# Layer 0 of a Strassen-tiled cross network: one fused VectorE instruction for the state, and product 3 cut into seven

## The chip, the cores and the metric

The kernel runs on one core of a Trainium2 chip. The metric is the device time of one execution, in microseconds, as the median of several runs. Before the change it is 2269.24 us (three runs, 2269.07 to 2269.5). The engines are called by their names in the profile: PE is TensorE's matmul, PEld its weight load, DVE is VectorE, ACT is ScalarE, POOL is GpSimd, SP is SyncE, which here issues all DMAs.

## The reference

The inputs are x0 (16384 x 1024), six weight matrices ws (1024 x 1024 each) and six bias rows bs, all bfloat16. What is computed is

```python
x = x0
for l in range(6):
    proj = x @ ws[l] + bs[l]
    x = x0 * proj + x
```

In layer 0, x is x0, so the new state is x0 * proj + x0.

## The kernel before

**Tiles.** 1024 rows of x make a pair: two column blocks of 512 rows each, held transposed, features on partitions. A pair's state is one "big" tile (128 x 2 x 8 x 512: which of the two blocks, which of eight groups of 128 features, which row of the block). Eight sweeps (the loop over s) each take two pairs, side A and side B, through the six layers, in the order A0, B0, A1, B1 and so on: 96 steps. There are six big tiles: x0 of A and of B, the states of A and of B, and two for the next sweep's x0. "home" says which is which; they change roles at each sweep.

**Products.** A step multiplies the pair by a layer's weights as one level of a Strassen-Winograd scheme: seven products of half matrices, numbered 1 to 7, instead of eight. Each half product is 16 matmuls with 512 columns (4 row tiles by 4 of the contraction), in `mm`. The combined weights (5, 6, 7, 3) are made once, in sweep 0, by `combo` on VectorE, and stored to a DRAM tile Lc; from sweep 1 on they are loaded into a ring of nine weight tiles "wp" by `prefetch_upto`, on SP's queue. The combined activations are T13 (T5 and T7 in one tile), T2 (for product 6) and T4 (for product 4); each is a VectorE difference, in tiles of one buffer each.

**Products within products.** Product 2 in nearly all steps (`in2`) and product 4 from sweep 1 on (`in4`) are again cut in the same way: seven 256x256 products of four 256-column matmuls each, in `inner`. They need the differences of the activations (four VectorE instructions of 512 elements, `inner_t`, tiles ti2 and ti4, one buffer each) and of the weights (combo 8 for product 2, combo 9 for product 4, each four VectorE instructions of 512 elements and a store to Lc). Their partial results leave PSUM through ScalarE casts (`evi`) into ea, eb (product 2) and e4, e5 (product 4), and VectorE adds them up: for product 4 `s4` (two of 512 elements) and one of 2048 that adds E4 to C2.

**PSUM and ScalarE.** There are two pools of four PSUM banks, "px"; their roles change each step. Bank after bank is evicted by ScalarE, in program order: a cast (`acopy`) or an activation with the bias (`abias`), into P1s, P5s, S53, U2s (one buffer each) and C2 ("cb", two buffers). A new use of a bank waits for the eviction of the old one. In products 2 and 4, and between P1, P6 and P7, matmuls go on adding to a bank that ScalarE has read in between.

**The state.** A quarter of a new state is product sum times x0, plus the old state. So a quarter costs VectorE a multiplication and an addition (`fin_of`, 2048 elements each); the last two quarters (C2) are done in one multiplication and one addition of 4096 elements. The first quarter is made at the end of its own step (m0, a0). The others are the trail: they are done on VectorE at the head of the next step, between that step's own T2, T4 and ti4 (`trail`; the names in the loop are m1, s11, a1, s4, e4, mC2, aC2). s11 adds P5s to a half of C2, which is the last read of P5s. Before the step ends VectorE also makes ti2 of the other side (j02, j1, j3).

**Order.** `pin` keeps VectorE's, ScalarE's and SP's instructions in the order in which the program makes them. The matmuls are not pinned; the scheduler may interleave those of neighbouring products. In sweep 0 the weights are combined between the other work: in step A0 `combo(0, 8)` and `combo(0, 9)`, in step B0 those of layer 1. A `combo` on "ti4" uses the same single buffer as the activations' ti4.

**SP's queue.** Loads of weights wait for a free slot of the ring. At the end of a sweep, `turn_pair` transposes a state by DMA into the pair's old x0 tile and `write_pair` stores it, two DMAs of 1 MB; these stand in `pending`, which is issued at the head of a step after the prefetches.

Of the kernel before, what the change touches and what calls it, by code (L numbers as in the profile page):

```python
# [8 lines left out]
ADD = mybir.AluOpType.add  # L9
# [8 lines left out]
def kernel(  # L18
# [26 lines left out]
    def vtt(out, in0, in1, op):  # L45
        return pin(nc.vector.tensor_tensor(out=out, in0=in0, in1=in1, op=op))  # L46

    def vcopy(out, in_):
        return pin(nc.vector.tensor_copy(out=out, in_=in_))

# [25 lines left out]
    def bank(p):  # L76
        return p.tile([P, NB], FP32, name="px")

    Lc = dram.tile([L, 6, P, KH * H], BF16, name="Lc")
    CIDX = {5: 0, 6: 1, 7: 2, 3: 3, 8: 4, 9: 5}  # L80
    lc = lambda l, pid: Lc[l, CIDX[pid]].rearrange("p (k e) -> p k e", k=KH)

    def raw_src(l, pid):
# [38 lines left out]
    def combo(l, pid):  # L122
        if pid <= 7:
            a, op, b = {5: (lambda: raw12[l], ADD, lambda: W[0, l, 4]), 6: (lambda: W[0, l, 5], SUB, lambda: W[0, l, 1]),
                        3: (lambda: W[0, l, 2], SUB, lambda: W[0, l, 6]), 7: (lambda: W[0, l, 1], SUB, lambda: raw12[l])}[pid]
            if pid == 5:
                W[0, l, 5] = ei_pool.tile([P, KH, H], BF16, name=("eb", "e4")[l % 2])
            t = W[0, l, pid]
            vtt(t[:], a()[:], b()[:], op)
        else:  # L130
            w = W[0, l, {8: 2, 9: 4}[pid]]
            t = W[0, l, 8] if pid == 8 else ti_pool.tile([P, KH, H], BF16, name="ti4")
            i11, i12, i21, i22 = w[:, 0:2, 0:HE], w[:, 0:2, HE:H], w[:, 2:4, 0:HE], w[:, 2:4, HE:H]
# [5 lines left out]
        pin(nc.sync.dma_start(lc(l, pid), t[:]))  # L139
# [4 lines left out]
    def inner_t(hold, src, name):  # L144

        def t02():
            ti = ti_pool.tile([P, 4, 2, NQ], BF16, name=name)
# [12 lines left out]

        return [t02, t1, t3]
# [39 lines left out]
    make_identity(nc, ident[:])  # L201
    b_rows = const.tile([LK, P], BF16, name="b_rows")
    b_all = const.tile([P, LK], FP32, name="b_all")
    ones = const.tile([P, P], BF16, name="ones")
    signs = const.tile([P, P], BF16, name="signs")
    nc.vector.memset(ones[:], 0.0)
    nc.vector.memset(ones[0:1, :], 1.0)
    nc.vector.memset(signs[:], 0.0)
    nc.vector.memset(signs[0:2, :], 1.0)
    nc.vector.memset(signs[0:1, :], -1.0)  # L210
# [50 lines left out]
    def trail(Y, store):  # L261

        if Y is None:
            return [None] * 7
        C2, E4, e5 = Y.C2, Y.E4, Y.e5
        eh1 = lambda t: t[:, :, KH:KD, :]
        m1, a1 = fin_of(Y, Y.C12, 0, 1)

        def s4():
            for i in range(2):  # L270
                vtt(E4[:, 2 * i:2 * i + 2, NQ:NB], E4[:, 2 * i:2 * i + 2, (1 - i) * NQ:(2 - i) * NQ], e5[:], ADD)

        def a1s():
            a1()
            if store:
                store_half(Y, 0)

        return [m1, lambda: vtt(C2[:, 1], C2[:, 1], Y.P5s[:], ADD), a1s,
                s4 if E4 is not None else None,
                (lambda: vtt(C2[:, 0], C2[:, 0], E4[:], ADD)) if E4 is not None else None,  # L280
                lambda: vtt(C2[:], C2[:], eh1(Y.x0T), MULT),
                lambda: vtt(eh1(Y.xst), C2[:], eh1(Y.src_in), ADD)]

    def fin_of(Y, C, eh, n):
        xs = half(eh)
        return [lambda: vtt(C, C, Y.x0T[:, n, xs, :], MULT),
                lambda: vtt(Y.xst[:, n, xs, :], C, Y.src_in[:, n, xs, :], ADD)]

# [39 lines left out]
    for s in range(NPAIR // 2):  # L328
        for l in range(L):
            for side in ("A", "B"):  # L330
                X, Y = cur[side], prev
                first, last = step == 0, (X.pr, l) == LAST
                in2, in4 = not first, s > 0 and not (s + 1 == NPAIR // 2 and l + 1 == L)
                psA, psX = ps[step % 2], ps[1 - step % 2]
                step += 1
                bias = lambda eh, m, l=l: b_all[:, l * KD + eh * KH + m: l * KD + eh * KH + m + 1]
                if l == 0:
                    if side == "A" and s > 0:
                        home = dict(xA=home["nA"], xB=home["nB"], sA=home["sA"], sB=home["sB"], nA=home["xA"], nB=home["xB"])
                    X.xst = bigt(home["s" + side])  # L340

                def bring(who, s=s, home=home):
                    pr = 2 * (s + 1) + (who == "B")
# [9 lines left out]
                if s + 1 == NPAIR // 2 and side == "A" and l == 2:  # L353
                    x0R = bigt(home["nA"])[:].rearrange("p n k b -> p (n k b)").rearrange("p (j d) -> p j d", d=D)
                    xsR = bigt(home["nB"])

                    def load_rows():
                        pin(nc.sync.dma_start(brow[:], bs[L - 1].rearrange("(h e) -> h e", h=2)))
                        pin(nc.sync.dma_start(x0R, x0[B - PR:B, :].rearrange("(j p) d -> p j d", p=P)))

                    brow = zero[0:2, :]
                    pending.append(load_rows)

                def end_of(Y, late):
                    if s + 1 == NPAIR // 2 and side == "A" and l == L - 1 and not late:
# [19 lines left out]
                def mm(pid, wt, pts, m, start):  # L385
                    rhs = X.rhs(pid)
                    if last:
                        pt = pts[m][:]
                        if pid == 1:
                            nc.tensor.matmul(pt, lhsT=ones[:], rhs=zero[:], start=True, stop=False)  # L390
                        elif pid == 7:
                            nc.tensor.matmul(pt, lhsT=signs[:], rhs=zero[:], start=False, stop=False, skip_group_check=True)
# [30 lines left out]
                m1, s11, a1, s4, e4, mC2, aC2 = trail(Y, ended and last)  # L423
                if not first:
                    X.T13()
                P1s = evt("P1s")
# [11 lines left out]
                for f in (m1, s11, a1, t2, s4, t4, e4, i02, mC2, i1, aC2, i3):  # L438
                    if f is not None:
                        f()  # L440
                if in2:
                    q2, q5, q1 = bank(psX), bank(psX), bank(psX)
                    w2i = weights(8)
# [44 lines left out]
                    ev(P5s, pX, 3)  # L488
                    ev(S53, pX, 0, 0)
                    ev(P1s, pA, 3, 0)  # L490
                    for m in range(1, KH):
                        mm(3, w3, pX, m, False)
                        ev(S53, pX, m, 0)
# [57 lines left out]
                if s == 0:  # L551
                    if side == "A":
# [20 lines left out]
                X.C2, X.P5s, X.l = C2, P5s, l  # L573
                if in4:
                    w4, w4i, w7 = weights(4), weights(9), weights(7)
                    wj, wr4 = w4i[:].rearrange("p k (j e) -> p k j e", e=HE), sub_w(w4, HE)
# [15 lines left out]
                    inner(cols(z1), wj[:, 1], t4[:, 1], False)  # L592
                    evi(e4[0, 1], z1)
                    mm(6, w6, pA, 3, False)
                    ev(U2s, pA, 3)
                    mm(7, w7, pA, 0, False)
                    ev(C2[:, 1], pA, 0, 1)
                    inner(cols(z1), wj[:, 3], t4[:, 2], False)
                    evi(e4[1, 0], z1)
                    for m in range(1, KH):  # L600
                        mm(7, w7, pA, m, False)
                        ev(C2[:, 1], pA, m, 1)
                    col = lambda m0, j, pA=pA: (lambda m: pA[m0 + m][:, j * NQ:(j + 1) * NQ])
                    inner(col(0, 0), wr4[1, 0], b4[1, 0], False)
                    inner(col(0, 1), wj[:, 2], b4[1, 1], False)
# [80 lines left out]
```

## Time and profile before

| | |
|---|---|
| median of 3 runs | 2269.24 us |
| profiled execution | 2269.03 us, of which span 2267.3 us |
| instructions in the span | 33559 |
| TensorE matmul | busy 2259.1 us, 12925 instructions |
| VectorE | busy 2160.6 us, 2394 instructions |
| ScalarE | busy 1909.8 us, 3307 instructions |
| DMA | 334.59 MB, mean 148 GB/s |
| granted TensorE clock | 1.00 |

The profile is one execution. Times of instructions lie on an axis that begins with the span. A line of a timeline gives start, length, engine, source line, operation, output and inputs, shape, how many, and in brackets how long the engine was idle before it and who ended that. [...] Matmuls are pipelined: a 512-column matmul is 379 ns long, and the next starts 216 ns after it. VectorE's `vtt`, ScalarE's `acopy` and `abias` are helpers, so that all their instructions carry one line (46, 52, 55); the tiles' names tell them apart.

### The profile page before, as it was taken

How to read it: one execution, taken by the hardware profiler on the slowest of the kernel's cores; microseconds unless marked ns; L12 is line 12 of the kernel's file. 1: busy time of each engine (PE TensorE's matmuls, PEld its weight loads, DVE VectorE, ACT ScalarE, POOL GpSimd, SP SyncE). 2: the span in 40 equal slices, each digit the busy share in tenths (PEclk: the TensorE clock that was granted, in tenths of full speed). 3: DMA queues.
4: the chain of work that ended last, by engine and by line, in shares of the span. 5: the costliest groups of instructions: out<-in, count | busy, mean ns of one | idle time of the engine just before them, and what ended most of it. 6: DMA issues, size and time to landing. Idle time of an engine off the chain costs nothing.

```text
span 2267.3 us, 33559 instructions
## 1 busy us (share of the span) xinstructions
PE 2259.1 (100%) x12925; PEld 1264.3 (56%) x12925; DVE 2160.6 (95%) x2394; ACT 1909.8 (84%) x3307; POOL 0.7 (0%) x6
## 2 busy tenths in 40 slices
PE   9999999999999999999999999999999999999998
PEld 4555555555555555555555555555555555555554
DVE  8999989999999999999999999999999999999998
ACT  6777788888888888888888888888888888888886
POOL 0000000000000000000000000000000000000000
PEclk9999999999999999999999999999999999999999
DMA  7423495523944249442494434944348453583337
GB/s 232 149 94 121 148 212 165 144 85 121 254 137 130 93 123 256 133 121 100 128 256 121 121 115 128 242 121 123 124 127 232 121 131 121 131 223 121 107 117 177
DMA packets 508452, 334.59 MB, mean 148 GB/s; under 512 B 390530, under 2 KB 470404, under 8 KB 508292
## 3 DMA queue, kind: packets, MB, share of 16 engines
q1 hardware_dynamic: 508292, 332.45, 52.2%
q8 instruction: 101, 1.65, 0.3%
q14 instruction: 59, 0.48, 0.1%
HBM read 213.92 MB, written 52.43 MB: 117 GB/s over the span
## 4 chain that ended last, share of the span: by engine, by line
PE 98%; DVE 1%; DMA 0%; SPq 0%; issue 0%; ACT 0%; DVEq 0%
PE px L400 74%; PE px L408 24%; DMA wp<-in_ws_dram 0%; PE px L395 0%; DVE cb L46 0%; DVE S L46 0%; DVE P1s L46 0%; SPq L120 0%; DVE eb L46 0%; DVE T L46 0%; SPq L217 0%; PE px L390 0%; DVE wp L46 0%; ACT S L52 0%; SPq L220 0%
## 5 line engine op out<-in xcount | busy, mean ns | idle before, releaser
L400 PEld LDWEIGHTS <-wp 128*128 128x128 bf16 x7344 | 718.5, 98 | 669.8 <-issue 0.7
L400 PE MATMUL px<-T,wp 128*128 128x512 bf16 x4384 | 1069.4, 379 | 0.0
L400 PE MATMUL px<-big,wp 128*128 128x512 bf16 x2960 | 712.3, 379 | 0.4 <-ACT big L52 0.4
L408 PEld LDWEIGHTS <-wp 128*128 128x128 bf16 x4752 | 465.0, 98 | 254.3
L55 ACT ACTIVATE cb<-px,b_all 128x512 bf16<-128x512 f32 x760 | 501.6, 686 | 85.5 <-PE px L400 71.4
L408 PE MATMUL px<-ti,wp 128*128 128x256 bf16 x2684 | 402.6, 273 | 0.0
L52 ACT CAST ea<-px 128x512 bf16<-128x512 f32 x344 | 201.6, 586 | 140.5 <-PE px L408 140.5
L46 DVE TENSOR_TENSOR T<-big 128x4096 bf16<-128x4096 bf16 (+1 forms) x97 | 220.1, 2269 | 71.0 <-PE px L400 71.0
L52 ACT CAST U2s<-px 128x512 bf16<-128x512 f32 x384 | 224.9, 586 | 64.9 <-PE px L400 61.3
L55 ACT ACTIVATE P1s<-px,b_all 128x512 bf16<-128x512 f32 x380 | 253.9, 694 | 5.9 <-PE px L400 4.3
L55 ACT ACTIVATE S<-px,b_all 128x512 bf16<-128x512 f32 x380 | 242.0, 702 | 0.8 <-PE px L400 0.8
L46 DVE TENSOR_TENSOR T<-big,T 128x2048 bf16<-128x2048 bf16 x192 | 234.0, 1219 | 1.4
L52 ACT CAST P5s<-px 128x512 bf16<-128x512 f32 x384 | 218.3, 597 | 17.6 <-PE px L400 17.5
L46 DVE TENSOR_TENSOR cb<-cb,big 128x4096 bf16<-128x4096 bf16 (+2 forms) x107 | 222.8, 2086 | 0.3
L46 DVE TENSOR_TENSOR big<-cb,big 128x4096 bf16<-128x4096 bf16 x95 | 217.2, 2286 | 0.5
L52 ACT CAST e<-px 128x512 bf16<-128x512 f32 x328 | 193.0, 588 | 0.0
L408 PE MATMUL px<-big,wp 128*128 128x256 bf16 x1084 | 162.6, 273 | 0.0
L52 ACT CAST eb<-px 128x512 bf16<-128x512 f32 x258 | 152.1, 590 | 6.9 <-PE px L408 0.4
L408 PE MATMUL px<-T,wp 128*128 128x256 bf16 x984 | 134.2, 273 | 0.0
L46 DVE TENSOR_TENSOR P1s<-P1s,big 128x2048 bf16<-128x2048 bf16 x106 | 129.3, 1220 | 3.2 <-ACT P1s L55 2.4
L46 DVE TENSOR_TENSOR P1s<-P1s,ea 128x2048 bf16<-128x2048 bf16 x86 | 105.4, 1225 | 15.3 <-ACT P1s L55 3.7
L46 DVE TENSOR_TENSOR S<-U2s,S 128x2048 bf16<-128x2048 bf16 (+1 forms) x97 | 117.2, 1208 | 2.5 <-ACT U2s L52 2.4
(76 smaller groups left out, 1370.9 us busy)
## 6 DMA issues: line engine op xcount, KB each, us to landing
wp<-Lc SPq DMA_DIRECT2D x252, 512.0 KB, 4.7
wp<-in_ws_dram SPq DMA_DIRECT2D x144, 512.0 KB, 3.6
out_dram<-big SPq DMA_DIRECT2D x28, 1024.0 KB, 11.0
Lc<-big SPq DMA_DIRECT2D x15, 512.0 KB, 2.7
Lc<-wp SPq DMA_DIRECT2D x9, 512.0 KB, 2.7
ea<-in_ws_dram SPq DMA_DIRECT2D x6, 512.0 KB, 5.4
Lc<-ti SPq DMA_DIRECT2D x6, 512.0 KB, 3.2
big<-in_x_dram SPq DMA_DIRECT2D x1, 2048.0 KB, 10.6
```

Of the source, the lines that this page charges most:

```text
L46: return pin(nc.vector.tensor_tensor(out=out, in0=in0, in1=in1, op=op))
L52: return pin(nc.scalar.copy(out=out, in_=in_))
L55: return pin(nc.scalar.activation(out=out, in_=in_, func=IDENT, bias=bias, scale=1.0))
L400: nc.tensor.matmul(pts[m][:], lhsT=wt[:, k, m * P:(m + 1) * P], rhs=rhs[:, k, :], start=(start and k == 0), stop=(k == KH - 1), **kw)
L408: nc.tensor.matmul(dst(m), lhsT=w[:, k, m * P:(m + 1) * P], rhs=rhs[:, k, :], start=(start and m == 0 and k == 0), stop=(k == 1), skip_gro ...
```

## The change

It has five parts.

1. In layer 0 each multiplication and addition of the state becomes one VectorE instruction, `one_plus`: (C + 1) * x0, of 2048 elements a quarter. The C2 quarters, before one pair of instructions of 4096 elements, are two instructions of 2048. The second of them (mC0) is put off to the end of the next step where that is a layer-0 step.
2. Product 3 of layer 0, from sweep 1 on (`in3`, 14 steps), becomes seven 256x256 products. The new state's tile is not yet written then; three of its quarters hold what the cut needs: ti3 (xst[:, 0] second half), the combined weights w3i (xst[:, 1] second half, of side A, read by both sides), and the partial results E3 (xst[:, 1] first half). e6 is a new small tile. Two products are added in the product-3 place, one after product 6's first bank; the other four lie among products 6 and 7, in two new PSUM tiles y1 and y5 of the pool that holds product 3's banks, with four more ScalarE casts.
3. VectorE makes ti3 in the step (k02, k1, k3: four instructions of 512 elements), and E3's sums at the head of the next step, in front of the fused second quarter (two of 512, one of 2048).
4. In sweep 0, step A0, a new `combo(0, 10)` combines the weights of product 3: four VectorE instructions of 512 elements in a "ti4" tile, and a store to Lc, which is seven tiles a layer now. In each later sweep w3i is loaded by SP at the head of step A0, ahead of what else is pending.
5. The constant rows ones and signs, used in the last step alone, are no longer set by VectorE at the start but by POOL in the last step of side A, in a "ti4" tile.

```diff
+    def one_plus(out, c, x):
+        return pin(nc.vector.scalar_tensor_tensor(out=out, in0=c, scalar=1.0, in1=x, op0=ADD, op1=MULT))
...
-    CIDX = {5: 0, 6: 1, 7: 2, 3: 3, 8: 4, 9: 5}
+    CIDX = {5: 0, 6: 1, 7: 2, 3: 3, 8: 4, 9: 5, 10: 6}
...
-            w = W[0, l, {8: 2, 9: 4}[pid]]
+            w = W[0, l, {8: 2, 9: 4, 10: 3}[pid]]
...
-    ones = const.tile([P, P], BF16, name="ones")
-    signs = const.tile([P, P], BF16, name="signs")
-    nc.vector.memset(ones[:], 0.0)
...
+        if Y.E3 is not None:
+            def m1(E3=Y.E3, e6=Y.e6, C=Y.C12, mul=m1):
+                for i in range(2):
+                    vtt(E3[:, 2 * i:2 * i + 2, NQ:NB], E3[:, 2 * i:2 * i + 2, (1 - i) * NQ:(2 - i) * NQ], e6[:], ADD)
+                vtt(C, C, E3, ADD)
+                mul()
...
-                lambda: vtt(C2[:], C2[:], eh1(Y.x0T), MULT),
-                lambda: vtt(eh1(Y.xst), C2[:], eh1(Y.src_in), ADD)]
+                (lambda: one_plus(eh1(Y.xst)[:, 0], C2[:, 0], eh1(Y.x0T)[:, 0])) if Y.l == 0 else
+                (lambda: vtt(C2[:], C2[:], eh1(Y.x0T), MULT)),
+                None if Y.l == 0 else (lambda: vtt(eh1(Y.xst), C2[:], eh1(Y.src_in), ADD)),
+                (lambda: one_plus(eh1(Y.xst)[:, 1], C2[:, 1], eh1(Y.x0T)[:, 1])) if Y.l == 0 else None]
...
     def fin_of(Y, C, eh, n):
         xs = half(eh)
+        if Y.l == 0:
+            return [lambda: one_plus(Y.xst[:, n, xs, :], C, Y.x0T[:, n, xs, :]), None]
...
+                X.l, in3 = l, l == 0 and s > 0
...
+                    if in3 and side == "A":
+                        w3i = X.xst[:, 1, KH:KD, :]
+                        pending.insert(0, lambda w=w3i: pin(nc.sync.dma_start(w, lc(0, 10))))
...
+                if s + 1 == NPAIR // 2 and side == "A" and l == L - 1:
+                    rowsel = ti_pool.tile([P, 4, 2, NQ], BF16, name="ti4")
+                    ones, signs = rowsel[:, 0, 0, 0:P], rowsel[:, 1, 0, 0:P]
+                    nc.gpsimd.memset(rowsel[:, 0:2, 0, 0:P], 0.0)
...
+                if in3:
+                    ti3 = X.xst[:, 0, KH:KD, :].rearrange("p q (k b) -> p q k b", k=2)
+                    k02, k1, k3 = inner_t(X, lambda: X.rhs(3), "ti3", ti3)
+                for f in (m1, s11, a1, t2, k02, s4, k1, t4, k3, e4, i02, mC2, i1, aC2, i3):
...
-                    mm(3, w3, pX, 0, False)
-                    mm(5, w5, pX, 3, True)
...
+                    if in3:
+                        wk, wr3 = w3i.rearrange("p k (j e) -> p k j e", e=HE), sub_w(w3, HE)
+                        b3, t3 = sub4(X.rhs(3)), X.ti3
+                        colx = lambda m0, j, pX=pX: (lambda m: pX[m0 + m][:, j * NQ:(j + 1) * NQ])
+                        inner(colx(0, 0), wr3[1, 0], b3[1, 0], False)
+                        mm(5, w5, pX, 3, True)
+                        inner(colx(0, 1), wk[:, 2], b3[1, 1], False)
+                        ev(P5s, pX, 3)
+                        ev(P1s, pA, 3, 0)
+                        ev(S53, pX, 0, 0)
+                        ev(S53, pX, 1, 0)
...
+                        if l == 0:
+                            combo(l, 10)
...
                     mm(6, w6, pA, 0, False)
+                    if in3:
+                        inner(colx(2, 0), wr3[1, 1], t3[:, 3], False)
                     ev(U2s, pA, 0)
+                    if in3:
+                        ev(S53, pX, 2, 0)
+                        ev(S53, pX, 3, 0)
+                        y5, y1 = bank(psX), bank(psX)
+                        X.E3 = X.xst[:, 1, 0:KH, :]
+                        X.e6 = ei_pool.tile([P, 2, NQ], BF16, name="e6")
+                        e3 = sub4(X.E3)
                     inner(cols(z1), wr4[0, 0], b4[0, 0], True)
                     evi(e4[0, 0], z1)
...
+                    if in3:
+                        inner(cols(y1), wr3[0, 0], b3[0, 0], True)
+                        evi(e3[0, 0], y1)
...
+                    if in3:
+                        inner(cols(y5), wk[:, 0], t3[:, 0], True)
+                        evi(X.e6[:], y5)
...
+                    if in3:
+                        inner(cols(y1), wk[:, 1], t3[:, 1], False)
+                        evi(e3[0, 1], y1)
...
+                        if in3 and m == 1:
+                            inner(cols(y1), wk[:, 3], t3[:, 2], False)
+                            evi(e3[1, 0], y1)
+                    if mC0 is not None:
+                        mC0()
```

More of the change, by code (lines that the diff above doesn't have):

```diff
@@ L77, in bank @@
         return p.tile([P, NB], FP32, name="px")
-    Lc = dram.tile([L, 6, P, KH * H], BF16, name="Lc")
-    CIDX = {5: 0, 6: 1, 7: 2, 3: 3, 8: 4, 9: 5}
+    Lc = dram.tile([L, 7, P, KH * H], BF16, name="Lc")
+    CIDX = {5: 0, 6: 1, 7: 2, 3: 3, 8: 4, 9: 5, 10: 6}
     lc = lambda l, pid: Lc[l, CIDX[pid]].rearrange("p (k e) -> p k e", k=KH)
@@ L142, in sub4, with inner_t @@
         return {(i, j): t[:, 2 * i:2 * i + 2, j * NQ:(j + 1) * NQ] for i in range(2) for j in range(2)}
-    def inner_t(hold, src, name):
+    def inner_t(hold, src, name, tile=None):
         def t02():
-            ti = ti_pool.tile([P, 4, 2, NQ], BF16, name=name)
+            ti = tile if tile is not None else ti_pool.tile([P, 4, 2, NQ], BF16, name=name)
             setattr(hold, name, ti)
@@ L203 @@
     b_all = const.tile([P, LK], FP32, name="b_all")
-    ones = const.tile([P, P], BF16, name="ones")
-    signs = const.tile([P, P], BF16, name="signs")
-    nc.vector.memset(ones[:], 0.0)
[L207 to L210, printed above, removed]
     home = dict(xA=0, xB=1, sA=2, sB=3, nA=4, nB=5)
@@ L263, in trail @@
         if Y is None:
-            return [None] * 7
+            return [None] * 8
         C2, E4, e5 = Y.C2, Y.E4, Y.e5
@@ L267, in trail @@
         m1, a1 = fin_of(Y, Y.C12, 0, 1)
+        late_c = None
+        if Y.E3 is not None:
[4 more added lines that the diff above has]
+                mul()
         def s4():
@@ L273, in a1s @@
         def a1s():
-            a1()
+            if a1 is not None:
+                a1()
             if store:
@@ L362 @@
                     pending.append(load_rows)
+                if s + 1 == NPAIR // 2 and side == "A" and l == L - 1:
+                    rowsel = ti_pool.tile([P, 4, 2, NQ], BF16, name="ti4")
+                    ones, signs = rowsel[:, 0, 0, 0:P], rowsel[:, 1, 0, 0:P]
+                    nc.gpsimd.memset(rowsel[:, 0:2, 0, 0:P], 0.0)
+                    nc.gpsimd.memset(ones[0:1, :], 1.0)
+                    nc.gpsimd.memset(signs[0:2, :], 1.0)
+                    nc.gpsimd.memset(signs[0:1, :], -1.0)
                 def end_of(Y, late):
@@ L389, in mm @@
                         if pid == 1:
-                            nc.tensor.matmul(pt, lhsT=ones[:], rhs=zero[:], start=True, stop=False)
+                            nc.tensor.matmul(pt, lhsT=ones, rhs=zero[:], start=True, stop=False)
                         elif pid == 7:
-                            nc.tensor.matmul(pt, lhsT=signs[:], rhs=zero[:], start=False, stop=False, skip_group_check=True)
+                            nc.tensor.matmul(pt, lhsT=signs, rhs=zero[:], start=False, stop=False, skip_group_check=True)
                         for k in range(KH):
@@ L422 @@
                 ended = Y is not None and Y.l == L - 1
-                m1, s11, a1, s4, e4, mC2, aC2 = trail(Y, ended and last)
+                m1, s11, a1, s4, e4, mC2, aC2, mC0 = trail(Y, ended and last)
                 if not first:
@@ L437 @@
                 i02, i1, i3 = inner_t(X, lambda: X.T[4], "ti4") if in4 else [None] * 3
-                for f in (m1, s11, a1, t2, s4, t4, e4, i02, mC2, i1, aC2, i3):
+                X.E3 = None
+                k02, k1, k3 = [None] * 3
+                if in3:
+                    ti3 = X.xst[:, 0, KH:KD, :].rearrange("p q (k b) -> p q k b", k=2)
+                    k02, k1, k3 = inner_t(X, lambda: X.rhs(3), "ti3", ti3)
+                for f in (m1, s11, a1, t2, k02, s4, k1, t4, k3, e4, i02, mC2, i1, aC2, i3):
                     if f is not None:
                         f()
+                if not in3 and mC0 is not None:
+                    mC0()
+                    mC0 = None
                 if in2:
@@ L485 @@
                     w3 = weights(3)
-                    mm(3, w3, pX, 0, False)
-                    mm(5, w5, pX, 3, True)
[L488 to L493, printed above, removed]
+                    if in3:
[9 more added lines that the diff above has]
+                        ev(S53, pX, 1, 0)
+                    else:
+                        mm(3, w3, pX, 0, False)
+                        mm(5, w5, pX, 3, True)
+                        ev(P5s, pX, 3)
+                        ev(S53, pX, 0, 0)
+                        ev(P1s, pA, 3, 0)
+                        for m in range(1, KH):
+                            mm(3, w3, pX, m, False)
+                            ev(S53, pX, m, 0)
                     vtt(e0(EA), e0(EA), e0(EB), ADD)
@@ L572 @@
                 C2 = cb_pool.tile([P, 2, KH, NB], BF16, name="cb")
-                X.C2, X.P5s, X.l = C2, P5s, l
+                X.C2, X.P5s = C2, P5s
                 if in4:
@@ L602 @@
                         ev(C2[:, 1], pA, m, 1)
+                        if in3 and m == 1:
+                            inner(cols(y1), wk[:, 3], t3[:, 2], False)
+                            evi(e3[1, 0], y1)
+                    if mC0 is not None:
+                        mC0()
                     col = lambda m0, j, pA=pA: (lambda m: pA[m0 + m][:, j * NQ:(j + 1) * NQ])
```

## The prediction

> **What bounds the kernel now.** I read the page's busy row first, then the chain that ended last (its shares, then its pieces in order of time), then the windows and VectorE's waits, then timelines of a step and of the first 50 us. The first fence has the busy row, the shares of the chain, and four pieces of it (start, length, what).
>
> ```profile
> PE 2259.1 (100%) x12925; PEld 1264.3 (56%) x12925; DVE 2160.6 (95%) x2394; ACT 1909.8 (84%) x3307; POOL 0.7 (0%) x6
> PE 98%; DVE 1%; DMA 0%; SPq 0%; issue 0%; ACT 0%; DVEq 0%
> ...
> 256.56 17.27 PE px L400 x80
> 280.33 17.27 PE px L400 x80
> ...
> 327.49 5.18 PE px L400 x24
> 350.87 5.18 PE px L400 x24
> ```
>
> TensorE is the chain. The same place of a step recurs every 23.77 us in sweep 0 (280.33-256.56) and every 23.38 us later (350.87-327.49). The later steps have product 4 cut into seven, so the trace prices such a cut on TensorE: 0.40 us a step, if everything around it keeps up. Four 512-column matmuls follow each other in 0.865 us, four of 256 columns in 0.435 (below: 1402.37, 1402.81, 1403.67).
>
> ```profile
> 1167.00:1190.40 23.40, 23.40 (x138) 13.32 (x136) 22.45 (x26) 20.11 (x36) 0.00 (x0) 1.00 0.87 276
> DVE T L46 <- PE px L400: 71.0, 85, 1.6
> ```
>
> The first line is one window of a step's length (length, then busy time of TensorE, its weight loads, VectorE, ScalarE), the second VectorE's longest group of waits (total, times, longest). In a step VectorE works 22.45 of 23.40 us and ScalarE 20.11. VectorE's only regular pause is at T13, 71.0/85 = 0.84 us. So VectorE has 0.95 us to give per step.
>
> **TensorE's own gain.** Product 3 takes 16 x 0.216 = 3.46 us; seven 256x256 products take 7 x 0.435 = 3.04. Gain 0.41 us in each of 14 steps (layer 0, sweeps 1 to 7): -5.7 us.
>
> **ScalarE and the PSUM banks.** Each such step has four more evictions (y1 three times, y5 once; a cast follows a cast by 0.48 us), 1.9 us more, so 22.0 of 23.4. That fits as a mean, but banks come free in sequence (timelines of TensorE and of ScalarE around product 5's last bank):
>
> ```profile
> 1402.37 0.60 PE L408 MATMUL px<-ti,wp 128*128 128x256 bf16 x4
> 1402.81 1.03 PE L400 MATMUL px<-big,wp 128*128 128x512 bf16 x4
> 1403.67 1.03 PE L400 MATMUL px<-T,wp 128*128 128x512 bf16 x4
> ...
> 1403.01 0.59 ACT L52 CAST ea<-px 128x512 bf16<-128x512 f32 x1 [0.71 <-PE px L408]
> 1404.73 0.59 ACT L52 CAST P5s<-px 128x512 bf16<-128x512 f32 x1 [0.16 <-PE px L400]
> ```
>
> Product 5's last bank is the one that the cast at 1403.01 empties (till 1403.60, seen some 0.04 later). Now product 3's first bank, 0.86 us, lies between. In the changed order only four small matmuls and one large do, 0.65: a stall of 0.18. Next, the four banks of product 3 were evicted behind 2.6 us of its matmuls. Now 1.73 us after product 5 ends TensorE wants the bank of S53's first quarter for z1. That eviction starts after a cast (0.48) and P1s's (0.57), beginning 0.20 after product 5, lasts 0.69 and is seen 0.04 later: 1.98, a stall of 0.25. y1 needs S53's third bank, at 3.60 by the same sum, and comes at 3.50: 0.10. Together 0.53 us a step, more than the 0.41 gained: 14 x 0.53 = +7.4.
>
> **VectorE, the fused instruction.** The trace has no two-operation instruction; the nearest rows of the groups by form (count, busy us, mean ns):
>
> ```profile
> L46 DVE TENSOR_TENSOR T<-big,T 128x2048 bf16<-128x2048 bf16 x192 | 234.0, 1219 | 1.4
> L46 DVE TENSOR_TENSOR cb<-cb,big 128x4096 bf16<-128x4096 bf16 x95 | 217.0, 2285 | 0.0
> L46 DVE TENSOR_TENSOR ti<-T 128x512 bf16<-128x512 bf16 x164 | 61.8, 419 | 0.0
> L49 DVE CAST big<-px 128x512 bf16<-128x512 f32 x4 | 2.7, 689 | 7.5 <-PE px L242 7.5
> ```
>
> 512, 2048 and 4096 elements at 419, 1219, 2285 ns are 0.15 us plus 0.52 ns an element; in a row they follow each other 0.335, 1.135, 2.20 apart. The cast, 689, is 1.04 ns an element. Ends for 2048 elements: 1.22 us, or 2.29. The fused one does two operations an element, and by the rows' price per operation (0.52) that is 1.04, the slow row too. I take 2.20 us apart; 1.135 stays as a rival. So each pair of 2048 (2 x 1.135) becomes 2.20, a gain of 0.07 only, and the pair of 4096 (4.41) becomes 4.40. [...]
>
> Added on VectorE: four 512s for ti3 (1.34) in each layer-0 step; for E3 two 512s (0.67) and one 2048 (1.135) at the head of the next step. Where one reads the result just before it, add 0.1 (1408.64 to 1409.16 where 0.42 would do). Base work 22.55 with one such gap. Step A: 22.55+1.34-0.07+0.1 = 23.9, against TensorE's 23.38-0.41+0.53 = 23.50: late by 0.4. Step B has A's E3 as well: 22.55+1.34+1.81-0.15+0.35 = 25.9, so T13 of the step after it is 0.4+2.4 = 2.8 late. There P5s decides (timelines of one step: VectorE, ScalarE, TensorE):
>
> ```profile
> 1415.98 2.29 DVE L46 TENSOR_TENSOR T<-big 128x4096 bf16<-128x4096 bf16 x1 [0.84 <-PE px L400]
> 1419.32 1.22 DVE L46 TENSOR_TENSOR cb<-cb,P5s 128x2048 bf16<-128x2048 bf16 x1
> 1424.31 0.60 ACT L52 CAST P5s<-px 128x512 bf16<-128x512 f32 x1
> 1425.09 0.59 ACT L52 CAST ea<-px 128x512 bf16<-128x512 f32 x1 [0.17 <-PE px L408]
> 1425.75 0.60 PE L408 MATMUL px<-ti,wp 128*128 128x256 bf16 x4
> ```
>
> ScalarE rewrites P5s 8.33 us after T13 starts (1415.98 to 1424.31); VectorE must have read it. With E3 and the fused sum in front, that read ends at 2.8 + 2.20 (T13) + 0.77 and 1.26 (E3) + 2.20 (fused) + 1.22 = 10.45: ScalarE waits 2.1. Behind it is the cast of ea, which had 0.30 in hand, and the product at 1425.75, 0.07. TensorE stalls 1.75 us in layer 1's first step of each sweep, some 1.5 in sweep 1, where ti2 is made later: 6 x 1.75 + 1.5 = +12.0. T13 itself has 3.6 in hand, and the rest recovers by 0.84 a step.
>
> **The new store in sweep 0.** Combo 10 takes the one "ti4" buffer from combo 9, whose store to Lc must have landed; the wait stands in the built program on VectorE, so what is queued behind it (the S53 sum, T13 of the next step, all of its trail) waits too. Here: SP's timeline, the DMA view of the first stretch (size, us to landing), then VectorE's and TensorE's timelines.
>
> ```profile
> 30.45 0.32 SPq L139 DMA_DIRECT2D Lc<-ti  x1
> Lc<-ti SPq DMA_DIRECT2D x1, 512.0 KB, 10.2
> 30.38 2.28 DVE L46 TENSOR_TENSOR T<-big 128x4096 bf16<-128x4096 bf16 x1
> 38.07 1.03 PE L400 MATMUL px<-T,eb 128*128 128x512 bf16 x4
> ```
>
> The store goes out at 30.45 and lands 10.2 us later behind a full queue, at 40.65. Then combo 10 (4 x 0.335 + 0.2), the sum (1.135) and T13 (2.29): 45.7. TensorE wants T13 at 38.07: +7.65. T13 in hand, the fused sum and P5s's read (2.20+1.22) end 0.9 after ScalarE wants P5s (2.46 after product 5 begins): +0.55. VectorE then has 22.2 us of work to the end of the next T13 (T2 and T4 2.4; two fused 4.4; ea, eb and P1s 2.2; ti2 and a fused one 3.6; layer 1's combos 6.2; the sum and T13 3.4), 71.2; TensorE is there at 61.84+8.2 = 70.0: +1.2, and +0.55 again. Together +9.95.
>
> **At nothing.** The load of combo 10 (each sweep, half a MB) goes in SP's queue ahead of two output stores, waits for the turned pair, which the stores wait for anyway, and is read some 9 us into the step; the loads issued near there (857 us) landed after 7.1 us, the median of three. If it came later, each us costs up to 7. The memsets of ones and signs, now on POOL, lie a whole step ahead of their use; VectorE's, at the start, lay beside the first load. Weights 3 are held some 5 us longer; their slot is next read some 18 us after that, against those 7.1.
>
> **Sum.** -5.7 + 7.4 + 12.0 + 9.95 = +23.65 us, on the profiled execution's 2269.03 (span 2267.3 and 1.7 around), which is 0.2 below the median 2269.24: 2293.
>
> **Rivals.** (1) TensorE keeps its gain: the banks come free in time, fused sums keep VectorE in step, and the store has landed: 2269.2-5.7 = 2263.5. It decides where ScalarE's eviction after product 5 is 0.25 us earlier and VectorE under 23 us a step; 20.11 of 23.40 speaks for it, the order of the banks and 10.2 us against it. (2) The fused form runs at 1.22 us: VectorE's late steps shrink by 4 x 1.07 and the P5s stalls vanish, those of ScalarE (+7.4) and the store (+7.65) stay: 2269.2-5.7+15.05 = 2278.5. (3) The slow form, but the store lands as fast as that group's median (3.2 us): combo 10 fits in T13's 5.4 us in hand, some 1.7 stays: 2285.
>
> **How the numbers follow.** Forecast 0.80 (2293, own range 2286 to 2299); (2) 0.12, (3) 0.04, (1) 0.03, no change 0.01 (fast form, store early). Range 2283 to 2299: forecast and (3), 0.84, less a little for a stall mis-sized by over 0.9 us a sweep. About 0.2% (4.5 us) is what a measurement can tell: faster 0.03, same 0.02, slower 0.95.
>
> **What would show it.** Fused rows at 2.29 us (or 1.22); VectorE idle some 10 us near 30 to 41 us behind a DMA; a P5s wait of ScalarE near 2 us in each sweep's layer 1, TensorE idle 1.75 us; gaps of 0.18, 0.25 and 0.10 in layer-0 steps. The prediction is wrong if fused rows are near 1.2 us, if VectorE is not held at combo 10, or if TensorE waits for the new weight load.

## The result, and the profile after

The changed kernel takes 2310.98 us (median of five runs, 2308.98 to 2314.62) against 2269.35 before (five runs, 2269.07 to 2269.5): a ratio of 1.0186, interval 1.0175 to 1.0197. It is slower, as forecast, but by 41.6 us and not by 23.65; the forecast was 2293 and its range ended at 2299. The profiled execution is the fastest of the five, 2308.98, with a span of 2307.2.

First the busy row of the page and the shares of the chain that ended last, after the change.

```profile
PE 2264.8 (98%) x13093; PEld 1280.6 (56%) x13093; DVE 2205.5 (96%) x2459; ACT 1929.2 (84%) x3363; POOL 1.6 (0%) x10
PE 82%; DVE 11%; DMA 4%; SPq 1%; issue 1%; ACT 1%; DVEq 0%
```

TensorE was 98% of the chain and is 82%; VectorE took 11% of it and DMA 4%. The waits of the kernel after say where (total, times, longest): the largest of TensorE, then one of VectorE, then one of ScalarE.

```profile
PE px L428 <- DMA big<-Lc: 13.3, 6, 3.8
PE px L428 <- ACT ea L55: 9.6, 7, 1.8
PE px L420 <- DVE T L46: 8.2, 2, 6.9
...
PE px L428 <- DVE big L46: 0.9, 1, 0.9
PE px L428 <- DVE ti L46: 0.7, 1, 0.7
...
DVE ti L46 <- DMA Lc<-ti: 10.8, 1, 10.8
...
ACT P5s L55 <- DVE cb L46: 12.9, 8, 2.1
```

Line two is the forecast's P5s stall, and the 6.9 in line three is its late T13 in sweep 0. Line one is TensorE waiting six times for the load of combo 10, which the forecast put at nothing. Lines four and five are one place, in sweep 1.

A wait in that list counts only the time in which an engine stood. To account for all of the 39.95 us between the two profiled executions (2308.98 - 2269.03), I took the distance from each matmul's start to the next and subtracted its pace (0.216 us for 512 columns, 0.109 for 256). At half pace, as the table calls it, matmuls of 512 columns follow each other at 0.427 us.

| | us after, less before | forecast |
|---|---|---|
| pace of the whole stream (2254.5 before, 2248.9 after) | -5.6 | -5.7 |
| PSUM banks of product 3 not yet evicted (0.18, 0.27, 0.13 in a full step) | +6.2 | +7.4 |
| P5s, layer 1's first step (1.95, then 6 x 1.465) | +10.7 | +12.0 |
| sweep 0: T13 late by 7.10, later 0.09 and 0.53 | +7.7 | +9.95 |
| sweep 0: matmuls at half pace behind the 7.10 | +1.9 | 0 |
| load of combo 10, sweeps 2 to 7 (2.41, 2.05, 2.06, 1.77, 2.02, 3.94) | +14.25 | 0 |
| matmuls at half pace behind the 3.94 | +2.6 | 0 |
| sweep 1, side B: ti3 late (1.02 and 0.86) | +1.9 | 0 |
| first microseconds | +0.2 | 0 |

The rows add up to 39.85. The four forecast terms come to 19.0 where 23.65 was expected; 20.65 come from places where nothing was expected (and 0.2 from the start).

**The fused instruction** took the slow rate (2.29 us; the second rival had 1.22). Groups by form, after:

```profile
L49 DVE SCALAR_TENSOR_TENSOR big<-cb,big 128x2048 bf16<-128x2048 bf16 x32 | 73.0, 2285 | 0.0
L49 DVE SCALAR_TENSOR_TENSOR big<-S,big 128x2048 bf16<-128x2048 bf16 x16 | 36.7, 2291 | 0.5
L49 DVE SCALAR_TENSOR_TENSOR big<-P1s,big 128x2048 bf16<-128x2048 bf16 x16 | 36.6, 2285 | 0.0
```

2285 ns for 2048 elements is what a two-tensor instruction takes for 4096 (cb<-cb,big: 2285 ns before, 2286 after).

**Sweep 0.** Timelines of SP, VectorE and TensorE, after, and two windows (length, then busy time of TensorE, weight loads, VectorE, ScalarE, POOL; then the granted clock):

```profile
29.96 0.32 SPq L142 DMA_DIRECT2D Lc<-ti  x1
...
40.44 0.76 DVE L46 TENSOR_TENSOR ti<-wp 128x512 bf16<-128x512 bf16 x2 [10.84 <-DMA Lc<-ti]
...
43.05 2.28 DVE L46 TENSOR_TENSOR T<-big 128x4096 bf16<-128x4096 bf16 x1
...
45.39 1.89 PE L420 MATMUL px<-T,eb 128*128 128x512 bf16 x4 [6.94 <-DVE T L46]
```

```profile
44.00:52.00 8.00, 6.61 (x30) 3.61 (x31) 7.90 (x6) 2.45 (x5) 0.00 (x0) 0.67 0.01 5
2023.00:2029.00 6.00, 5.39 (x18) 2.63 (x19) 5.03 (x7) 2.19 (x4) 0.00 (x0) 0.51 1.14 262
```

The store of combo 9 goes out at 29.96 and VectorE stands till 40.44. T13 comes at 45.3, and TensorE goes on at 45.39. Then its four matmuls of 512 columns take 1.89 us where four of them took 1.03: the clock granted in that window is 0.67, and 0.51 in the one behind the longest wait for the load.

**The P5s stall** (timelines of VectorE, ScalarE, TensorE in sweep 3, after):

```profile
923.93 2.29 DVE L46 TENSOR_TENSOR T<-big 128x4096 bf16<-128x4096 bf16 x1
926.13 0.76 DVE L46 TENSOR_TENSOR big<-big,e 128x512 bf16<-128x512 bf16 x2
926.92 1.23 DVE L46 TENSOR_TENSOR S<-S,big 128x2048 bf16<-128x2048 bf16 x1
928.18 2.29 DVE L49 SCALAR_TENSOR_TENSOR big<-S,big 128x2048 bf16<-128x2048 bf16 x1
930.39 1.22 DVE L46 TENSOR_TENSOR cb<-cb,P5s 128x2048 bf16<-128x2048 bf16 x1
...
931.64 0.59 ACT L55 CAST P5s<-px 128x512 bf16<-128x512 f32 x1 [1.66 <-DVE cb L46]
932.12 0.59 ACT L55 CAST ea<-px 128x512 bf16<-128x512 f32 x1
...
932.76 0.60 PE L428 MATMUL px<-ti,wp 128*128 128x256 bf16 x4 [1.30 <-ACT ea L55]
```

This is the chain that the forecast drew: E3's sums and the fused sum stand before the read of P5s (930.39), ScalarE's cast waits for that read, the cast of ea stands behind it, and TensorE waits for ea.

**The load.** SP's and TensorE's timelines at the head of sweep 3, after:

```profile
864.40 11.15 SPq L326 DMA_TRANSPOSE big<-big  x1
875.65 0.52 SPq L102 DMA_DIRECT2D wp<-Lc  x1
...
877.77 0.39 SPq L352 DMA_DIRECT2D big<-Lc  x1
878.21 8.43 SPq L333 DMA_DIRECT2D out_dram<-big  x2
...
882.75 0.38 PE L428 MATMUL px<-big,wp 128*128 128x256 bf16 x2
885.01 0.39 PE L428 MATMUL px<-big,big 128*128 128x256 bf16 x2 [1.88 <-DMA big<-Lc]
```

SP is busy for 11.15 us with issuing the transposition, then for 2.1 with four ring loads, and reaches the load at 877.77. It lands 7.2 us later, at 884.97. TensorE wants it at 882.97.

### The profile page after: what moved, and what is told of

It reads as the page before. It is cut to its first block, busy times and chain, and to the rows that moved or that the text cites. A ratio compares the mean times of both kernels' runs of the same rounds, so it can differ in the third digit from the quotient of the medians.

```text
span 2307.2 us, 34008 instructions
## 1 busy us (share of the span) xinstructions
PE 2264.8 (98%) x13093; PEld 1280.6 (56%) x13093; DVE 2205.5 (96%) x2459; ACT 1929.2 (84%) x3363; POOL 1.6 (0%) x10
## 4 chain that ended last, share of the span: by engine, by line
PE 82%; DVE 11%; DMA 4%; SPq 1%; issue 1%; ACT 1%; DVEq 0%
PE px L420 61%; PE px L428 20%; DVE big L49 4%; DVE T L46 2%; DMA big<-Lc 2%; DVE cb L46 1%; DMA big<-big 1%; DVE S L46 1%; DVE big L46 1%; DVE ti L46 1%; DVE P1s L46 1%; DMA Lc<-ti 0%; SPq L219 0%; SPq L224 0%; PE px L415 0%
## 5 line engine op out<-in xcount | busy, mean ns | idle before, releaser
L420 PE MATMUL px<-T,wp 128*128 128x512 bf16 x4384 | 1083.9, 379 | 0.2
L420 PE MATMUL px<-big,wp 128*128 128x512 bf16 x2736 | 659.2, 379 | 0.4 <-ACT big L55 0.4
L428 PE MATMUL px<-ti,wp 128*128 128x256 bf16 x2684 | 402.6, 273 | 10.7 <-ACT ea L55 9.6
L55 ACT CAST e<-px 128x512 bf16<-128x512 f32 x342 | 204.3, 606 | 0.3 <-PE px L428 0.3
L428 PE MATMUL px<-big,wp 128*128 128x256 bf16 x1252 | 190.7, 273 | 0.9 <-DVE big L46 0.9
L46 DVE TENSOR_TENSOR cb<-cb,big 128x4096 bf16<-128x4096 bf16 (+2 forms) x91 | 186.4, 2052 | 0.3
L46 DVE TENSOR_TENSOR big<-cb,big 128x4096 bf16<-128x4096 bf16 x79 | 180.6, 2286 | 0.4
L46 DVE TENSOR_TENSOR cb<-cb,P5s 128x2048 bf16<-128x2048 bf16 (+1 forms) x97 | 117.2, 1208 | 0.0
```

Of the source, the lines that this page charges most:

```text
L55: return pin(nc.scalar.copy(out=out, in_=in_))
L420: nc.tensor.matmul(pts[m][:], lhsT=wt[:, k, m * P:(m + 1) * P], rhs=rhs[:, k, :], start=(start and k == 0), stop=(k == KH - 1), **kw)
L428: nc.tensor.matmul(dst(m), lhsT=w[:, k, m * P:(m + 1) * P], rhs=rhs[:, k, :], start=(start and m == 0 and k == 0), stop=(k == 1), skip_gro ...
```

## The experiments

Two theories stood after the result. The one: the four forecast terms hold, the load is a fifth one, and its stalls and those at half pace add what is missing. The rival: the terms do not add; the load's waits and VectorE's lateness are the same time seen twice, or the store, the fused form or the banks were mis-sized, so that taking one away gives nothing, or more than its row.

**e1, no load.** Product 3 has no weights of its own.

```diff
-                    if in3 and side == "A":
-                        w3i = X.xst[:, 1, KH:KD, :]
-                        pending.insert(0, lambda w=w3i: pin(nc.sync.dma_start(w, lc(0, 10))))
...
-                        wk, wr3 = w3i.rearrange(...), sub_w(w3, HE)
+                        wk, wr3 = w2i[:].rearrange(...), sub_w(w3, HE)
```

> The changed kernel without the load of product 3's combined weights: product 3 reads combo 8's weight tile, already in the ring, in its place (so layer 0's product 3 is computed with other weights). Theory: the 17 us that the forecast lacks are this load. The trace shows TensorE waiting for it 14.25 us in six sweeps (1.8 to 3.9 each), and after the longest wait 2.6 us more at half the clock. Then this kernel takes 2311 - 17 = 2294 us (2291 to 2297), shows no wait on that DMA, and keeps the others: 7.1 us at the head, 1.5 us in layer 1 of each sweep. Rival: the load only covers a wait of product 3 for VectorE or for a PSUM bank that stands right behind it; then TensorE waits in the same place for something else and the time stays above 2304.

Measured: 2294.46 us (2293.84 to 2295.2), 1.011 of before (1.0095 to 1.0125). TensorE's waits in e1:

```profile
PE px L425 <- ACT ea L55: 11.2, 7, 1.6
PE px L417 <- DVE T L46: 8.7, 3, 7.4
```

With the load out, the time lies within 1.5 us of the forecast's 2293, and by its terms: pace -5.6, banks 14 x 0.58 = +8.1, P5s 1.81 + 6 x 1.755 = +12.3, sweep 0 7.60 + 1.57 at half pace + 0.39 + 0.53 = +10.1. The P5s stall is now the 1.75 of the forecast in sweeps 2 to 7. In the changed kernel it was 1.465, since the load held TensorE by some 2 us a step earlier, in which VectorE caught up a little. So the load is a cost of its own, some 16.5 us in the medians, with that small overlap.

**e2, a place of its own for combo 10** in sweep 0, so that it need not wait for combo 9's store.

```diff
-            t = W[0, l, 8] if pid == 8 else ti_pool.tile([P, KH, H], BF16, name="ti4")
+            t = W[0, l, 8] if pid == 8 else quarter(spare, 2) if pid == 10 else ti_pool.tile(...)
```

> The changed kernel with combo 10 in a free quarter of the spare big tile instead of the one ti4 buffer, so that VectorE does not wait for combo 9's store to land. Theory: the store costs 7.1 us of waiting, 1.9 us of matmuls at half the clock right after it, and 0.5 us at P5s in the next steps: 2311 - 9.5 = 2301.5 us (2299 to 2305). Rival: VectorE, at 23 of 23.8 us a step in sweep 0, pays combo 10's work later anyway, and less than 5 us comes back (over 2306).

Measured: 2303.35 (2300.0 to 2304.34), 1.0151 of before (1.0134 to 1.0168): 7.6 less than the changed kernel. TensorE's waits in e2:

```profile
PE px L428 <- DMA big<-Lc: 12.7, 6, 3.4
PE px L428 <- ACT ea L55: 9.6, 7, 1.8
...
PE px L420 <- DVE T L46: 1.4, 1, 1.4
```

The wait for T13 of 6.9 near 38 us is gone, and with it the half pace behind it and the two later stalls: the whole of the sweep-0 rows, 9.6 by the table. The profiled executions differ by 9.0 (2300.0 and 2308.98). The rest lies mostly in sweep 1, where ti3 keeps TensorE waiting 0.7 us longer. The waits for the load vary from sweep to sweep (here 1.52 to 3.58); with the half pace behind them they come to 17.0 us here and 16.85 in the changed kernel.

**e3, s11 ahead of E3's sums**, so that P5s is read before them.

```diff
-                for f in (m1, s11, a1, t2, k02, ...
+                for f in ((s11, m1) if Y is not None and Y.E3 is not None else (m1, s11)) + (a1, t2, k02, ...
```

> The changed kernel with one edit of order: where the step before had product 3 cut, VectorE does s11 (the last read of P5s) before E3's sums and the fused second quarter, not after them. Theory: P5s is what stalls layer 1's first step, 1.95 + 6 x 1.47 = 10.7 us; the read then comes 4.2 us sooner, ScalarE does not wait, and the time is 2311 - 10.7 = 2300 us (2297 to 2304). Rival: VectorE is 2.8 us behind there whatever the order, and another of its products (T13, ti4, S53) takes the place of P5s: over 2306.

Measured: 2303.99 (2301.12 to 2304.89), 1.015 (1.0135 to 1.0165): 7.0 less, not 10.7. The profiled executions, which the waits below and the sums behind them come from, differ by only 4.5 (2304.45 and 2308.98). TensorE's waits in e3:

```profile
PE px L428 <- DMA big<-Lc: 15.8, 6, 3.8
PE px L420 <- DVE T L46: 9.9, 4, 8.3
PE px L428 <- DVE big L46: 2.2, 1, 2.2
```

The P5s stalls are gone from TensorE altogether (no wait for ea is left among its largest). But the waits for the load grew: 14.25 to 16.74 by the distances, and 1.67 and 1.68 at half pace behind two of them where 2.6 was behind one; sweep 1's ti3 costs 1.4 more, sweep 0 1.35 more. So the order was the cause of the P5s stall, and its full 10.7 was there; some of what it gave went to other stalls. Why the load was later here I can't say from one trace.

**e4, the fused instruction alone**, in the kernel before, with product 3 whole: `one_plus` and its uses in `trail` and `fin_of` as in the change, and the second C2 quarter in the trail.

```diff
-                lambda: vtt(C2[:], C2[:], eh1(Y.x0T), MULT),
-                lambda: vtt(eh1(Y.xst), C2[:], eh1(Y.src_in), ADD)]
+                (lambda: one_plus(eh1(Y.xst)[:, 0], C2[:, 0], eh1(Y.x0T)[:, 0])) if Y.l == 0 else
+                (lambda: vtt(C2[:], C2[:], eh1(Y.x0T), MULT)),
...
```

> The kernel before with the fused instruction alone in layer 0 (one_plus for each quarter, the C2 half in two instructions of 2048), product 3 left whole. The trace of the changed kernel has the fused instruction at 2285 ns, against 2 x 1219 for the pair that it replaces. Theory: VectorE gets 0.15 us a layer-0 step, TensorE stays the bound: 2269.3 us, within 0.5 of before. Rival: the slow rate costs in itself, since a C2 half that was read in one pass of 4096 now comes in two and T or ti2 come later; then each of the 16 layer-0 steps would show a TensorE gap and the time would be 2271 or more.

Measured: 2269.19 (2268.71 to 2269.64, ten runs), 1.0 of before (0.999 to 1.0009). Its busy row:

```profile
PE 2259.0 (100%) x12925; PEld 1264.2 (56%) x12925; DVE 2159.4 (95%) x2362; ACT 1909.7 (84%) x3307; POOL 0.7 (0%) x6
```

32 instructions fewer, 1.2 us less work for VectorE, and no time: VectorE still waits some 0.83 us for TensorE at each T13 (70.9 us, 85 times). Alone the fused form is worth nothing.

**e5, the fused instruction undone**, on e1: each quarter has again a multiplication and an addition. The two C2 quarters are four instructions of 2048 elements, where the kernel before has two of 4096, so this is not quite the old form.

```diff
-        return pin(nc.vector.scalar_tensor_tensor(out=out, in0=c, scalar=1.0, in1=x, op0=ADD, op1=MULT))
+        vtt(c, c, x, MULT)
+        return vtt(out, c, x, ADD)
```

> The run without the load (2294.5 us), with the fused instruction undone: a multiplication and an addition of 2048 elements for each quarter, the second right behind the first. Theory: a pair in a row takes 2 x 1.135 + 0.1 against 2.20 us, and five pairs stand in the way of step B and of layer 1's first step: VectorE is some 0.5 to 1 us later there, P5s stalls 2.2 us and not 1.75 in each sweep and product 4's first steps wait once more for ti4: 2294.5 + 7 = 2301 us (2298 to 2304). Rival: the fused instruction brings or costs nothing, since 2285 ns is what the pair took: 2294 to 2296.

Measured: 2303.17 (2302.86 to 2304.24), 1.015 (1.0136 to 1.0164): 8.7 more than e1. Where VectorE is the late one, each 0.07 us that the form saves, and the gap of about 0.1 between two instructions of which the second reads the first's result, shows (in e5 such a pair starts 1.26 us apart, 1193.81 to 1195.07, where 1.135 would do). From the first P5s cast of a sweep to that of the next it is mostly 283.61 in e5 and 282.67 in e1; sweep 1 differs by 1.3, and sweep 4 of e5 has 1.7 more, at half pace. So the fused form does help inside this change, by the slow rate and not by the fast one.

**e9, the cut without VectorE's work and without the load**: what the cut alone gives TensorE and costs ScalarE.

```diff
-                    ti3 = X.xst[:, 0, KH:KD, :].rearrange("p q (k b) -> p q k b", k=2)
-                    k02, k1, k3 = inner_t(X, lambda: X.rhs(3), "ti3", ti3)
+                    X.ti3 = X.x0T[:, 0, KH:KD, :].rearrange("p q (k b) -> p q k b", k=2)
...
-        if Y.E3 is not None:
+        if False:
```

The load is left out as in e1 and combo 10 has a place as in e2.

> Product 3 cut into seven as in the change, but without what the cut asks of VectorE and of the DMA queue: no load (combo 8's weights are read), ti3 replaced by a part of x0, E3's partial results evicted but not added up, and combo 10 in a place of its own. So layer 0's product 3 is left wrong; TensorE and ScalarE do all they do in the change. It prices the first two terms of the forecast: TensorE's gain of 5.7 us against 14 x 0.53 = 7.4 us of waits for PSUM banks. Theory: 2269.2 - 5.7 + 7.4 = 2271 us (2270 to 2272.5), with gaps of 0.18, 0.25 and 0.10 in each layer-0 step and nothing else. Rival: the bank waits show only because VectorE is late and holds ScalarE up; without its extra work they go and the gain stays: 2263.5 to 2265.

Measured: 2271.73 (2271.41 to 2274.32, ten runs), 1.0012 (1.0003 to 1.0021), 2.4 more than before. TensorE's timeline in e9 at the place of the second and third gap:

```profile
1149.79 0.59 PE L417 MATMUL px<-T,wp 128*128 128x512 bf16 x2
1150.49 0.60 PE L425 MATMUL px<-T,wp 128*128 128x256 bf16 x4
...
1151.79 0.38 PE L417 MATMUL px<-T,wp 128*128 128x512 bf16 x1
1152.14 0.60 PE L425 MATMUL px<-big,wp 128*128 128x256 bf16 x4
```

Two 512-column matmuls begun at 1149.79 would let the next start at 1150.22; it starts at 1150.49 (0.27). One begun at 1151.79 would let it start at 1152.01; it starts at 1152.14 (0.13). With the 0.18 before them that is 0.58 a step against the 0.40 that the cut gives: 14 x 0.18 = 2.5. A layer-0 step lasts 23.56 us in e9 and 23.38 before. Even with all else free, the cut in this order loses.

**e7, the load earlier in SP's queue**: behind the transposition as before, but ahead of the four ring loads.

```diff
+                        if side == "B" and s + 1 < NPAIR // 2:
+                            pre["xst"] = bigt(home["sA"])
+                            pin(nc.sync.dma_start(pre["xst"][:, 1, KH:KD, :], lc(0, 10)))
...
-                        pending.insert(0, lambda w=w3i: pin(nc.sync.dma_start(w, lc(0, 10))))
```

> The changed kernel with one DMA moved: the load of product 3's combined weights stands right behind the DMA that turns the old state out of that tile, ahead of four loads of the ring, not behind them. Theory: the load is late because it stands behind four loads that wait for ring slots and share the queue (issue 2 us after product 5 could use it, 7.3 us to land). Issued first it lands some 3 to 4 us after the turn, before TensorE needs it: the 14.25 us of waits and 2.6 us of half clock go, and P5s's stall grows by 0.3 a sweep as in the run without the load: 2295 us (2293 to 2298). Rival: SP then stands in its wait for the turn's landing, the four loads behind it come late, and TensorE waits for weights 6, 4, 9 or 7 instead: above 2304.

Measured: 2296.1 (2295.99 to 2298.77), 1.0118 (1.0102 to 1.0133): 14.9 less than the changed kernel. SP's timeline in e7, same place:

```profile
865.58 11.01 SPq L327 DMA_TRANSPOSE big<-big  x1
878.53 0.32 SPq L392 DMA_DIRECT2D big<-Lc  x1
878.95 0.38 SPq L102 DMA_DIRECT2D wp<-Lc  x1
```

No wait of TensorE for big<-Lc is left in e7. Product 5 of that step begins at 879.58, so the load goes out 1.05 us ahead of it (0.64 in the changed kernel), and is read at 884.13 without a wait: it landed in 5.6 us at most, where behind the ring loads it took 7.2. Of the 2.05 us that it was late, the issue accounts for 0.41 and the landing for the rest. That it lands sooner because the two megabytes of the ring loads no longer stand in front is likely, as nothing else was moved; no run varies their number. This is the load's price shown from the other side: the same work, one DMA moved. (The profiled execution is e7's slowest, 2298.77; in it sweep 1's ti3 kept TensorE waiting 2.5 us.)

**e8, all mended.** e2, e7 and e3 (e3 where it helps) together, and the orders of VectorE and ScalarE changed where a trace had shown a wait: in layer 0 product 6's first two banks are multiplied earlier, and ScalarE casts S53's banks 2 and 3 ahead of U2s's first, P5s's banks 1 and 2 ahead of ea[1,0], and P1s's last bank ahead of P5s's last; VectorE makes one of ti4's differences ahead of the fused C2 quarter, and T13 in halves in layers 1 and 2. Two of the edits:

```diff
-                    evi(ea[1, 0], q1)
+                    if not in3:
+                        evi(ea[1, 0], q1)
...
+                    if in3:
+                        evi(ea[1, 0], q1)
...
-                if not first:
+                if s > 0 and 1 <= l <= 2:
+                    X.T13(0)
+                    X.T13(1)
+                elif not first:
```

> The whole change with every wait mended that the traces name: combo 10 in its own place; the load right behind the turn; s11 ahead of E3's sums; ti4's second difference ahead of the fused C2 quarter; T13 in two halves in layers 1 and 2; and in layer-0 steps ScalarE's order changed so that P5s 1 and 2 come before ea's last cast, P1s 3 before P5s 3, S53 2 and 3 before U2s 0, with product 6's first two banks between product 5 and product 3. Theory: each wait has one cause and all are removed, so TensorE's 5.7 us come through, less some 0.2 us a sweep of T13: 2265 us (2263.5 to 2267). Rival: VectorE has 3 us a sweep too much, and as one wait is removed its debt shows at the next: 2270 or more.

Measured: 2268.93 (2267.23 to 2270.97, eleven runs), 0.9998 of before (0.999 to 1.0007). All that the change lost is back, 42 us; of the 5.6 that it was to gain, nothing that can be measured. The expected 2265 did not come. The largest waits of TensorE in e8:

```profile
PE px L423 <- DVE T L46: 1.7, 4, 1.0
PE px L233 <- DVE zero L203: 1.2, 1, 1.2
PE px L431 <- DVE ti L46: 0.4, 1, 0.4
PE px L423 <- ACT big L55: 0.4, 1, 0.4
```

The step from one first P5s cast to the next, in sweep 4, in us:

| kernel | A0 | B0 | A1 | B1 | A2 |
|---|---|---|---|---|---|
| before | 23.38 | 23.38 | 23.38 | 23.38 | 23.38 |
| after | 25.45 | 25.33 | 23.06 | 23.38 | 23.38 |
| e9 | 23.56 | 23.56 | 23.38 | 23.38 | 23.38 |
| e8 | 22.98 | 22.98 | 23.63 | 23.56 | 23.20 |

In e8 the two layer-0 steps are 0.40 shorter each, the whole gain of the cut. The three steps behind them are 0.25 longer together, so this sweep gains 0.55. So do sweeps 3 and 5; sweeps 6 and 7 gain 0.44 and 0.36, sweep 2 nothing, and sweep 1 loses 0.75. In the profiled executions e8 is 1.1 faster than before (2267.91 and 2269.03), less than its runs differ among themselves. In the layer-1 steps VectorE is all but full: it works 23.46 of 23.60 us in A1 and in B1 of sweep 4, and in A1 the 0.24 us for which TensorE stands is a wait for T13. This speaks for the debt that the rival named, though it cost less than the rival's 2270; no run takes work from VectorE in these steps.

## Why the prediction was wrong

**The step that failed** is the paragraph "At nothing", on the load of combo 10: it "is read some 9 us into the step; the loads issued near there (857 us) landed after 7.1 us". The 7.1 was right (7.2 measured), and so, nearly, were the 9 us. What it had wrong is the moment of issue: it let the load go out near the start of the step (in the trace of before product 1 begins at 855.53), but SP does not reach it there. It had been placed ahead of two output stores, and the trace of before shows when these are issued (SP's timeline, before):

```profile
858.52 2.05 SPq L99 DMA_DIRECT2D wp<-Lc  x2
860.67 8.74 SPq L325 DMA_DIRECT2D out_dram<-big  x2
```

So the load would go out at 860.67, 5.1 us into the step, and land at 867.8. Product 5 of that step begins at 860.73, and the load is read 4.55 us after that (in the trace after: 885.01 less the wait of 2.05, less product 5's start at 878.41): 865.3. It would be 2.5 us late, and the runs showed 1.8 to 3.9: six times, 14.25 us. The text itself named the price ("If it came later, each us costs up to 7") and the reading that would refute it ("if TensorE waits for the new weight load"), but took the cover for granted. e1 and e7 show that the load is the cause; with it gone or moved, 2294.46 and 2296.1 stand beside the forecast 2293. In the profiled executions the change costs 39.95 us, 16.3 more than forecast: the load and the half pace behind it add 16.85, half pace in sweep 0 and ti3 add 3.8, and the four forecast terms came to 4.65 less than expected.

**Half pace behind long stalls** (4.5 us in the profiled execution) was in no step: each stall was priced as the time that TensorE stands. The windows at clocks of 0.67 and 0.51 show it.

**ti3 in sweep 1** (1.9 us) was not seen either: VectorE's four instructions write into the old state's tile, whose transposition must have been read (VectorE waits 1.9 us, once, for the DMA big<-big).

What was right, and what was mis-sized:

- *TensorE's gain.* -5.7 forecast, -5.6 measured.
- *ScalarE and the banks.* 0.18, 0.25, 0.10 forecast; 0.18, 0.27, 0.13 measured. In e9, where nothing else stands in the way, the sum of gain and gaps is +2.4, forecast +1.7; so the gaps do not come from a late VectorE.
- *The fused instruction.* 2.29 us forecast from the nearest rows, 2285 ns measured. The fast rate, 1.22 us, is not borne out, and the second rival (2278.5) falls with it.
- *P5s.* 6 x 1.75 + 1.5 forecast; 6 x 1.755 + 1.81 in e1. In the changed kernel 6 x 1.465 + 1.95, since the load's wait gave VectorE time.
- *The store in sweep 0.* 7.65 forecast, 7.10 and (e1) 7.60 measured. Of the later pieces, 1.2 at the next T13 was 0.09 and 0.39, and the first 0.55 did not show, for the matmuls ran at half pace meanwhile: 1.86 and 1.57. In e1 the sum, 10.1, meets the 9.95 partly by luck: time at half pace stands where late pieces were forecast.

The first rival (2263.5) needed the banks free 0.25 us earlier and VectorE under 23 us a step. e8 reached the first by ScalarE's order, in the layer-0 steps, but not the second (23.46 in a layer-1 step), and the time did not follow. The third (2285) needed an early landing; it took 10.4 us (29.96 to 40.4).

## What to carry to other kernels

A transfer that "is hidden" has two ends: find when its queue reaches it (what stands in front, how long each holds the queue) and the first instruction that reads it; a distance from the start of a step is neither. Where one engine is at 100%, cutting its work by 0.4 us a step pays only if evictions, sums and loads in the same step have room in sequence, not in the mean: here the orders of ScalarE, VectorE and SP had to be redone to get no loss. And a stall on TensorE can cost more than its length: behind the 3.94 us one here matmuls at half pace took 2.6 us more, behind the 7.10 us one 1.9.

## What the runs showed that was not expected

**Half pace.** The traces record the clock that TensorE is granted. These are windows of the changed kernel, cut where that record changes or a multiple of 3.413 us from there (start and end, length, busy time of TensorE, weight loads, VectorE, ScalarE, POOL, then the granted clock):

```profile
882.06:885.47 3.41, 1.53 (x12) 0.91 (x11) 3.41 (x6) 1.74 (x4) 0.00 (x0) 1.00 1.06 352
885.47:888.89 3.42, 3.31 (x22) 1.96 (x21) 3.42 (x3) 2.15 (x4) 0.00 (x0) 1.00 1.28 290
...
2018.70:2022.11 3.41, 1.14 (x9) 0.58 (x6) 3.41 (x6) 1.80 (x4) 0.00 (x0) 1.00 0.97 350
2022.11:2028.94 6.83, 5.33 (x18) 2.57 (x19) 5.86 (x7) 2.13 (x4) 0.00 (x0) 0.50 1.13 269
```

In all ten traces the clock is whole or half, and it changes only at times that lie whole multiples of 3.413 us apart (in the changed kernel half clock lasts 6.83, two such windows, and the first whole stretch 37.55, eleven). How long TensorE stood within one window went with the clock of the next. From 27 us on, and short of the kernel's end, eleven windows at whole clock were followed by half clock; TensorE had stood 2.30 us or more in each, counted by distances as above (2.30, 2.39, 2.44, 2.44, 2.52, 2.68, and five times all of it). In every other window at whole clock it had stood 2.05 or less. So in these traces it mattered where a stall of 2 to 4 us fell: e3's stall of 2.88 was cut into 1.96 and 0.92 by the edge of a window and was not followed by half pace, its stall of 2.44 lay in one window and was. In e5 one of seven stalls of 2.03 was, the only one that lay whole in one window, with a wait of 0.27 behind it. What was lost is half of what was left of the half-clock windows when TensorE started again: 1.4 to 2.6 us in these traces. A window did not have to be idle throughout before half clock: 2.30 of its 3.41 us were enough. The traces show when the clock halves, not why.

**Spread.** Runs of the changed kernel lie within 5.6 us, of the kernel before beside them within 0.43. Their mean granted clocks go with their times: 0.997 at 2308.98, 0.996 at 2309.99 and 2310.98, 0.995 at 2312.51 and 2314.62. That the load's waits now bring half pace and now do not would explain much of it: a half-clock window lowers the mean by 0.0007 (half of 3.41 in 2310 us), so the difference of 0.002 is some three windows, and at most 1.7 us each some 5 us, an estimate from rounded clocks. Only one execution of each kernel has a trace, so this is argued.

**SP's own time.** Issuing one transposition of a state held SP's queue, and all that stood behind it, for 10.6 to 13.5 us (11.15 and 11.01 above, 10.64 and 13.54 near the same place of the kernel before).
